# One tuned kernel of an FFT, two linear layers and a routed expert layer: single fold additions given out per step, evictions of a group moved to one engine

## The chip, the cores and the metric

The kernel runs on one core of one Trainium2 chip. The metric is the device time of one execution in microseconds, the median of several runs. A separate execution was recorded by the hardware profiler; all rows below are from that one.

## The reference

The input `x` has 8 batches of 3072 positions by 256 features. Three stages follow each other:

```python
X = np.fft.fft(x, axis=1); X = np.fft.fft(X, axis=2); x = X.real.reshape(24576, 256)
a = x @ w1; b = x @ w2; x = ((a * b) @ w3) @ w_out          # 256 -> 1024 -> 1024 -> 256
logits = x @ w_gate                                         # 8 experts
# every expert takes its 3072 best tokens, in order of the logit
out[mask_e] = np.maximum(x[mask_e] @ e1[e], 0) @ e2[e]
```

All of it is single precision. The kernel keeps that accuracy with three matmuls for one product (high times high, high times low, low times high), so most tensors exist as a rounded high part and a low part that holds the rest.

## The kernel before, in words

The program has two stages. Stage A makes the FFT and the two linear layers and leaves the rows of `x` and the logits. Stage B chooses the tokens and runs the experts. The change touches stage A alone.

Stage A works in steps. A step is one `(batch, set, q, f)`: 8 batches, 2 sets of frequencies, 3 blocks `q` of 256 columns, 8 slices `f` of the 1024 features, so 48 steps a batch and 384 in all. In this text the steps of a batch are counted 0 to 47, and a *group* is the 8 steps of one `(batch, set, q)`; the steps with f = 2 are 2, 10, 18, 26, 34 and 42. In each step `front` (line 825) has TensorE (PE) write two accumulators in PSUM, `us` and `ue` (name `l`, four banks in all, so two steps' worth); the matmul L845 is the first that writes `ue`. ScalarE (ACT) copies `us` to `qs` (L849), VectorE (DVE) makes sum and difference `pm` (L851, L852), then their product (L868); ACT rounds the product to `ah` (L862), and GpSimd (POOL) makes the rest `al` (L863). Three steps later (`LAG`) PE multiplies `ah` and `al` with the combined second weights into four accumulators `acc` (L809, L810, L813), one bank each, over the 8 slices of the group. After the eighth slice, which falls on the next group's f = 2, the four banks are copied to SBUF (`xo`): banks 0 and 2 by ACT (L920), banks 1 and 3 by DVE (L921, because `EV` is 1). There is one set of `acc` banks, so the next group's first product waits for these copies. The last 8 groups (from step 32 of batch 6) are kept aside: there PE makes logits alone, two short matmuls a step.

Beside that, the *fold* of the next batch is given out piece by piece. `fold_batch` loads three tiles of the input and adds and subtracts reflected rows, on POOL, in pieces whose costs in us it yields; the loop lets it run while a credit, which gains `FOLD` = 1.3 a step, is positive. In the third tile (t = 2) four additions per side cross the two halves of the partitions; these `shifted` additions (L348 to L351, 64x128 each) are DVE's. Then `split` makes the high part (ACT, L373) and the low part (DVE, L374) of `FA` and `FB`, and from step 38 on PE reads `FA` for the next batch's first transform (`dft_set`, matmuls into `l` between the steps' own). `later(n, fn)` puts a piece off to the end of the n-th step from now, where `due()` gives it out.

The order on each engine is the order in which this Python code records it; nothing is rescheduled.

Of the kernel before, what the change touches and what calls it, by code (L numbers as in the profile page):

```python
# [213 lines left out]
def cp(eng, out, in_):  # L214

    return eng.dma_start(f32(out), f32(in_))
# [63 lines left out]
def stage_a(ctx, tc, I, nb, k):  # L280
    nc, vec, act, pool = k.nc, k.vec, k.act, k.pool
# [36 lines left out]
    def later(n, fn):  # L318
        if late is None or n == 0:
            fn()  # L320
        else:
            late.append([n, fn])
# [9 lines left out]
    def fold_rows(xt, t, cw, new, fe, wait=0):  # L332

        lo, hi = slice(0, 64), slice(64, 128)
        if xt is not None:
            xo = xt[:, :, 0]
            for z, op in ((fe, ALU.add), (xo, ALU.subtract)):
                for h in range(2):
                    g = slice(4 * h, 4 * h + 4)
                    pool.tensor_tensor(z[:, g], xt[:, g, 0], xt[:, g, 1], op=op)  # L340
                    yield 1.2
            sides = ((fe, ALU.add, ALU.subtract, ALU.add, 0), (xo, ALU.subtract, ALU.add, ALU.subtract, 2))
        else:
            sides = ((fe, ALU.add, ALU.subtract, ALU.add, 0),)

        def shifted(z, o, opx):
            a, b = (0, 1) if o == 0 else (1, 0)
            vec.tensor_tensor(FO[lo, o], z[lo, a], z[lo, a + 2], op=opx)  # L348
            vec.tensor_tensor(FO[hi, o], z[lo, b], z[lo, b + 2], op=opx)
            vec.tensor_tensor(FO[lo, o + 1], z[hi, a], z[hi, a + 2], op=opx)  # L350
            vec.tensor_tensor(FO[hi, o + 1], z[hi, b], z[hi, b + 2], op=opx)  # L351

        for z, op4, opx, opr, o in sides:
            pool.tensor_tensor(z[:, 0:4], z[:, 0:4], z[:, 4:8], op=op4)
            yield 1.2
            if z is fe:
                FO = new()
            if t < 2:
                pool.tensor_tensor(FO[:, o:o + 2], z[:, 0:2], z[:, 2:4], op=opx)
                yield 0.7  # L360
            else:
                later(wait, lambda z=z, o=o, opx=opx: shifted(z, o, opx))
            pool.tensor_tensor(z[:, 4:6], z[:, 0:2], z[:, 2:4], op=opr)
            yield 0.7
            r = 4 + o
            first, second = (ALU.subtract, ALU.add) if o == 0 else (ALU.add, ALU.subtract)
            pool.tensor_tensor(FO[:, r], z[:, 4], z[:, 5], op=first)
            yield 0.4
            pool.tensor_tensor(FO[:, r + 1], z[:, 4], z[:, 5], op=second)
            yield 0.4  # L370

    def split(hi, lo, src):
        act.activation(hi, src, AF.Copy)  # L373
        vec.tensor_tensor(lo, src, hi, op=ALU.subtract)  # L374
# [72 lines left out]
    def xplace(dt):  # L447
        return own.tile([128, 2080], dt, name="xt", bufs=2)[:, :2048]


    def fold_batch(b, F, wait=0):
        FA = [own.tile([128, 2, 6, 128], F32R, name=f"FA{i}") for i in range(2)]
        FB = [own.tile([128, 4, 3, 128], F32R, name=f"FB{i}") for i in range(2)]
        F[b] = FA, FB
        xts = []

        def rows():

            for hl in range(2):
                r = k.sp_d[2 + 3 * hl:5 + 3 * hl, b:b + 1].rearrange("h b d -> b h d")  # L460
                cp(nc.sync, FA[hl][0:1].rearrange("p x i d -> p (x i) d")[:, 1:7:5], r[:, 0:2])
                cp(nc.sync, FB[hl][0:1, 2, 0:1], r[:, 2:3])

        def load(t):
            xts.append(xplace(F32).rearrange("p (g h d) -> p g h d", g=8, h=2))
            nc.sync.dma_start(xts[t], I["xg"][b, :, t].rearrange("p g (h d) -> p g h d", h=2))

        load(0)
        if wait:
            load(1)  # L470
        else:
            yield load
        for t in range(3):
            xt = xts[t]
            fe = fold.tile([128, 8, 128], F32, name="fe")
            made = []

            def new():
                made.append(fold.tile([128, 8, 128], F32, name="FO"))
                return made[0]  # L480

            yield from fold_rows(xt, t, 128, new, fe, wait)
            FO = made[0]
            if t == 0:
                load(2)

            fa = FO[:, 0:4].rearrange("p (x i) d -> p x i d", x=2)
            later(wait + 1 if wait else 0, lambda t=t, fa=fa: split(FA[0][:, :, 2 * t:2 * t + 2], FA[1][:, :, 2 * t:2 * t + 2], fa))
            later(wait + 2 if wait else 0, lambda t=t, FO=FO: split(FB[0][:, :, t], FB[1][:, :, t], FO[:, 4:8]))
            if t == 0:  # L490
                later(wait + 2 if wait else 0, rows)

# [207 lines left out]
    def col_mm(st):  # L700
        for step in (dft_a(0, FA8, NB, sF, tmp) if st == 0 else dft_b(0, FB8, NB, sF, tmp, r8)):
            step()
        q = (nc.scalar, nc.sync)[st]
        if st == 1:
            x = xplace(F32R)
            ehs[1] = [x[:NB, i * 768:(i + 1) * 768] for i in range(2)]
        eh = ehs[st]
        split(eh[0], eh[1], sF[:NB, 0:768])
        if st == 1:
            split(r8m[0], r8m[1], sF[:NB, 769:770])  # L710
        for r, hl in ((0, 0), (1, 0), (2, 1)):
            cp(q, k.ed[st, :, r], eh[hl])
            if st == 1:
                cp(q, k.em[r].rearrange("(b o) -> b o", o=1), r8m[hl])
        if st == 1:
            for w in range(2):
                cp(q, mb3[32 * w:32 * w + 3], k.em)
# [7 lines left out]
    EOs, F, st0 = {}, {}, []  # L725

    with tc.manual_schedule(engines=ALL):
# [7 lines left out]
        fg = fold_batch(0, F)  # L735
# [134 lines left out]
    def number(g):  # L870

        b, st, q, f = g
        return b * 6 + st * 3 + q - (nb * 6 - k.aside)
# [90 lines left out]

    e3t, acct, gates = [None, None], [None], []
    steps = [(b, st, q, f) for b, st in sets for q in range(3) for f in range(NF)]
    LAG, FOLD, EV, AH, W8 = 3, 1.3, 1, 1, 1
    FOLD_AT = 3
    LAST = (7,)
    DFT_AT = {0: (1, 4, 7, 10), 1: (14, 16, 18, 20)}  # L970
    pend, todo, fg, credit, ahp = [], [], iter(()), 0.0, []
    mid = middle()
    with tc.manual_schedule(engines=ALL):
        for t in e3s:
            vec.memset(t.rearrange("p w c -> p (w c)").bitcast(F32), 0.0)
        for g in steps:
            b, st, q, f = g
            si, at = b * 2 + st, q * NF + f
            if st == 0 and at == FOLD_AT and b + 1 < nb:
                fg = fold_batch(b + 1, F, 2)  # L980
            nx = sets[si + 1] if si + 1 < len(sets) else None
            if nx and at == (DFT_AT[st][0] if (b, st) != (0, 0) else 5):
                if st == 1:
                    assert next(fg, None) is None, 'fold late'
                EOs[nx], todo = dft_set(nx[0], nx[1], F[nx[0]])
            fr = front(g)
            if (b, st, at) == (0, 0, 0):

                cut = 2 * (576 + 579) // 2 + 63
                pool.dma_start(tabB[:, :, :cut], I["tab"][:, :, C1N:C1N + cut])  # L990
                pool.dma_start(sg, I["sg"])
                pool.dma_start(tabB[:, :, cut:], I["tab"][:, :, C1N + cut:])
            if (b, st, at) == (0, 0, 4):
                col_mm(1)
            pend.append((g, fr))
            if len(pend) > LAG:
                back(*pend.pop(0))
            fr[3]()
            ahp.append(fr[2])
            if len(ahp) > AH:  # L1000
                ahp.pop(0)()
            due()
            credit = min(credit + FOLD, FOLD)
            while credit > 0:
                credit -= next(fg, 9.0)
            if (b, st) == (nb - 1, 1) and at in (2, 4, 6, 8, 10, 12, 22):
                next(mid)
            if (b, st, at) == (NB - 1, 0, 0):
                k.load_rcon()
            if number(g) == -3 and f == 0:  # L1010
                gates.append(work.tile([128, NF, 2 * E], F32R, name="gates", bufs=1))
                for i in range(2):
                    act.activation(gates[0][:, :, i * E:(i + 1) * E], W[i][:, :, D:], AF.Copy)
            if at in (DFT_AT[st] if (b, st) != (0, 0) else (5, 7, 9, 11)) and todo:
                todo.pop(0)(W8)
        for fn in ahp:
            fn()
        for p in pend:
            back(*p)
            due()  # L1020
        while late:
            due()
# [631 lines left out]
```

## Time and profile before

| | us |
|---|---|
| median of 3 runs (2855.15 to 2857.86) | 2857.8 |
| the profiled execution | 2851.39 |
| its span, first to last instruction | 2849.6 |
| PE busy | 2681.3 (94%) |
| DVE busy | 2156.5 (76%) |
| POOL busy | 1528.8 (54%) |
| ACT busy | 1307.3 (46%) |

The first step's L845 starts at 119.0 us and the last group ends near 1416 us; stage B takes the rest. Busy shares are means over both stages. Matmuls overlap each other, so PE counts as busy as long as one is under way; what can be won on PE in stage A are the holes between them, and those are what the waits of PE list.

### The profile page before, as it was taken

The page shows a single profiled execution, that of the slowest core. Times are in us where ns is not written, and L with a number is a line of the kernel's source. Part 1 is how long each engine was busy: PE and PEld are TensorE (multiplying, and loading weights), DVE is VectorE, ACT ScalarE, POOL GpSimd, SP SyncE. Part 2 cuts the span into 40 slices and gives each one's busy share as a digit, 9 for nine tenths or more (in the row PEclk, how much of TensorE's full clock was granted, in tenths as well). Part 3 has the DMA queues.
Part 4 walks back from the last instruction along what each step waited for, and adds up shares of the span by engine and source line. Part 5 has one row for each costly group of instructions (what it writes and reads, how often), then busy time and mean ns, then how long its engine had stood idle before and what let it go on. Part 6 is the DMA issues. An engine that isn't in the chain of part 4 may idle for free.

```text
span 2849.6 us, 52085 instructions
## 1 busy us (share of the span) xinstructions
PE 2681.3 (94%) x19967; PEld 2462.0 (86%) x19967; DVE 2156.5 (76%) x3888; ACT 1307.3 (46%) x2319; POOL 1528.8 (54%) x1537
## 2 busy tenths in 40 slices
PE   4899999999999999999897899989999999999998
PEld 2899999999999999987696788878888888889997
DVE  8787787977879787898878788788787878863222
ACT  2443433434344343444453656556474646533332
POOL 7385775847658494864403335353534445353532
PEclk8999999999999999999998999999999999999999
DMA  6311010100102010135385112121211212111211
GB/s 222 122 61 39 31 53 21 60 27 31 53 16 68 16 53 31 43 135 202 133 310 185 50 63 58 43 74 41 76 46 62 55 40 77 45 64 44 75 46 36
DMA packets 104709, 207.35 MB, mean 73 GB/s; under 512 B 35179, under 2 KB 60443, under 8 KB 99339
## 3 DMA queue, kind: packets, MB, share of 16 engines
q1 hardware_dynamic: 81000, 131.02, 13.6%
q0 software_dynamic: 22224, 72.58, 8.0%
q8 instruction: 158, 2.59, 0.4%
q14 instruction: 93, 0.75, 0.1%
q10 hardware_dynamic: 1234, 0.41, 0.1%
HBM read 118.15 MB, written 80.28 MB: 70 GB/s over the span
## 4 chain that ended last, share of the span: by engine, by line
PE 69%; DVE 21%; issue 4%; ACT 3%; POOL 2%; DMA 2%; DVEq 0%; another core or an unknown queue 0%; POOLq 0%; SPq 0%; ACTq 0%
PE yp L1491 14%; PE l L220 6%; PE l L222 6%; PE l L221 6%; PE hp L220 5%; PE hp L221 4%; PE hp L222 4%; PE acc L809 4%; PE acc L813 4%; PE acc L810 4%; DVE qs L868 3%; DVE oR L1094 3%; PE l L845 2%; DVE pm L851 2%; DVE pm L852 2%
## 5 line engine op out<-in xcount | busy, mean ns | idle before, releaser
L863 POOL TENSOR_TENSOR al<-qs,ah 128x512 fp32r<-128x512 f32 x376 | 515.6, 1371 | 421.3 <-ACT ah L862 336.4
L1491 PE MATMUL yp<-FA,W 128*128 128x256 f32 x3040 | 623.7, 287 | 19.6 <-DVE W L1474 9.6
L1491 PEld LDWEIGHTS yp<-FA,W 128*128 128x128 f32 x3040 | 499.3, 191 | 46.5 <-DVE W L1474 13.6
L868 DVE TENSOR_TENSOR qs<-pm 128x512 f32<-128x512 f32 x384 | 393.9, 1026 | 36.3 <-POOL al L863 0.9
L1474 DVE SCALAR_TENSOR_TENSOR W<-hp,W 128x512 fp32r<-128x512 f32 x336 | 230.1, 687 | 229.5 <-ACT W L1470 217.2
L851 DVE TENSOR_TENSOR pm<-l,qs 128x512 f32<-128x512 f32 x384 | 264.9, 690 | 174.1 <-PE l L222 143.6
L1491 PE MATMUL yp<-FB,W 128*128 128x256 f32 x1520 | 388.6, 282 | 0.0
L849 ACT ACTIVATE qs<-l 128x512 f32<-128x512 f32 x384 | 227.7, 593 | 347.6 <-PE l L222 325.3
L862 ACT ACTIVATE ah<-qs 128x512 fp32r<-128x512 f32 x376 | 236.8, 630 | 281.4 <-DVE qs L868 237.7
L220 PE MATMUL hp<-tabA,tabB 128*128 128x512 f32 x768 | 320.5, 417 | 0.9 <-ACT tabA L1440 0.9
L1470 ACT ACTIVATE W<-hp 128x512 fp32r<-128x512 f32 x336 | 197.3, 594 | 257.9 <-PE hp L222 237.9
L221 PE MATMUL hp<-tabA,tabB 128*128 128x512 f32 x768 | 305.0, 397 | 6.0 <-DVE tabA L1444 6.0
L1501 POOL DMA_INDIRECT out_dram<-yo,oi x188 | 189.4, 1007 | 225.4 <-DMA out_dram<-yo,oi 212.2
L1491 PEld LDWEIGHTS yp<-FB,W 128*128 128x128 f32 x1520 | 288.5, 190 | 14.5
L809 PE MATMUL acc<-W,ah 128*128 128x264 f32 x1120 | 285.6, 286 | 14.3 <-DVE xo L921 14.3
L810 PE MATMUL acc<-W,ah 128*128 128x264 f32 x1120 | 284.2, 284 | 0.0
L1094 DVE TENSOR_SCALAR_CACHE_REDUCE oR<-oR,nx 128x1536 uint16<-128x1536 uint16 x196 | 281.4, 1459 | 0.0
L852 DVE TENSOR_TENSOR pm<-l,qs 128x512 f32<-128x512 f32 x384 | 261.3, 680 | 0.0
L1465 POOL TENSOR_TENSOR W<-xo,W 128x512 fp32r<-128x512 f32 x48 | 66.6, 1387 | 352.9 <-ACT W L1463 334.9
L1415 POOL DMA_INDIRECT xt<-xs_d,idx x192 | 194.6, 1013 | 111.4 <-issue 50.8
L222 PE MATMUL hp<-tabA,tabB 128*128 128x512 f32 x624 | 247.1, 396 | 0.0
L809 PEld LDWEIGHTS acc<-W,ah 128*128 128x128 f32 x1120 | 211.1, 188 | 16.5 <-DVE xo L921 16.4
(368 smaller groups left out, 7042.4 us busy)
## 6 DMA issues: line engine op xcount, KB each, us to landing
xs_d<-xo SPq DMA_DIRECT2D x96, 260.0 KB
xt<-in_xg_dram SPq DMA_DIRECT2D x24, 1024.0 KB
away<-ah SPq DMA_DIRECT2D x56, 256.0 KB
away<-al SPq DMA_DIRECT2D x56, 256.0 KB
yo<-away SPq DMA_DIRECT2D x28, 512.0 KB
raw<-in_w3t_dram SPq DMA_DIRECT2D x16, 512.0 KB
FA<-away SPq DMA_DIRECT2D x14, 512.0 KB
FB<-away SPq DMA_DIRECT2D x14, 512.0 KB
```

Source lines behind the costliest of these rows:

```text
L220: nc.tensor.matmul(out, ah, bh, start=start, stop=False, skip_group_check=True)
L221: nc.tensor.matmul(out, ah, bl, start=False, stop=False, skip_group_check=True)
L222: nc.tensor.matmul(out, al, bh, start=False, stop=stop, skip_group_check=True)
L809: nc.tensor.matmul(acc[i][:, :264], ah[:, a], W[0][:, f], start=f == 0, stop=False, skip_group_check=True)
L810: nc.tensor.matmul(acc[i][:, :264], ah[:, a], W[1][:, f], start=False, stop=False, skip_group_check=True)
L851: vec.tensor_tensor(pm[:, 0].rearrange("p w c -> p (w c)"), ue, qs, op=ALU.add)
L852: vec.tensor_tensor(pm[:, 1].rearrange("p w c -> p (w c)"), ue, qs, op=ALU.subtract)
L862: act.activation(ah, qs, AF.Copy)
L863: (vec if n == k.aside - 1 and f in LAST else pool).tensor_tensor(al, qs, ah, op=ALU.subtract)
L868: return ah, al, parts, lambda: vec.tensor_tensor(ab, pm[:, :, 0], pm[:, :, 1], op=ALU.mult)
L1094: vec.tensor_scalar(jk[:, :n], T[:, :n], nx[:, i:i + 1], None, op0=ALU.is_ge, op1=ALU.add, accum_out=acc[:, i:i + 1])
L1491: nc.tensor.matmul(yp[i], hhl[seq[s][0]][:, t[i]], seq[s][1], start=f == 0 and s == 0 and (i % 2 == 0 or len(yp) == 4), stop=f == NF - 1 a ...
```

## The change

Three edits, all in stage A. The four shifted additions of a side are no longer one deferred piece but four, given out at the end of four successive steps, and the splits of the third tile come two steps later than before to stay behind them. `EV` becomes 0: ACT copies all four banks of a group. And the fold's credit is set to -4 x 1.3 when a batch's fold begins, so that it starts in the same step in each batch.

```diff
         def shifted(z, o, opx):
             a, b = (0, 1) if o == 0 else (1, 0)
-            vec.tensor_tensor(FO[lo, o], z[lo, a], z[lo, a + 2], op=opx)
-            vec.tensor_tensor(FO[hi, o], z[lo, b], z[lo, b + 2], op=opx)
-            vec.tensor_tensor(FO[lo, o + 1], z[hi, a], z[hi, a + 2], op=opx)
-            vec.tensor_tensor(FO[hi, o + 1], z[hi, b], z[hi, b + 2], op=opx)
+            for i, (to, of, c) in enumerate(((lo, lo, a), (hi, lo, b), (lo, hi, a), (hi, hi, b))):
+                later(wait and wait + i, lambda to=to, of=of, c=c, d=o + i // 2: vec.tensor_tensor(FO[to, d], z[of, c], z[of, c + 2], op=opx))
...
-                later(wait, lambda z=z, o=o, opx=opx: shifted(z, o, opx))
+
+                shifted(z, o, opx)
...
-            later(wait + 1 if wait else 0, lambda t=t, fa=fa: split(FA[0][:, :, 2 * t:2 * t + 2], FA[1][:, :, 2 * t:2 * t + 2], fa))
-            later(wait + 2 if wait else 0, lambda t=t, FO=FO: split(FB[0][:, :, t], FB[1][:, :, t], FO[:, 4:8]))
+            later(wait + (3 if t == 2 else 1) if wait else 0, lambda t=t, fa=fa: split(FA[0][:, :, 2 * t:2 * t + 2], FA[1][:, :, 2 * t:2 * t + 2], fa))
+            later(wait + (4 if t == 2 else 2) if wait else 0, lambda t=t, FO=FO: split(FB[0][:, :, t], FB[1][:, :, t], FO[:, 4:8]))
...
-    LAG, FOLD, EV, AH, W8 = 3, 1.3, 1, 1, 1
+    LAG, FOLD, EV, AH, W8 = 3, 1.3, 0, 1, 1
...
             if st == 0 and at == FOLD_AT and b + 1 < nb:
-                fg = fold_batch(b + 1, F, 2)
+                fg, credit = fold_batch(b + 1, F, 2), -4 * FOLD
```

Line numbers of the changed kernel are one lower from here on (L868 is L867). On PE the order of the instructions is the same as before. On DVE, in batch 0 from the product of step 31 on (`FO` is the fold's output, `fe` and `xt` its two sides, `pm` and `qs` the step's own), it was:

```order
L868 TENSOR_TENSOR qs_2257<-pm_2274 128x512
L348 TENSOR_TENSOR FO_2215<-fe_2002 64x128
L349 TENSOR_TENSOR FO_2215<-fe_2002 64x128
L350 TENSOR_TENSOR FO_2215<-fe_2002 64x128
L351 TENSOR_TENSOR FO_2215<-fe_2002 64x128
L851 TENSOR_TENSOR pm_2317<-l1_2302,qs_2300 128x512
L852 TENSOR_TENSOR pm_2317<-l1_2302,qs_2300 128x512
L868 TENSOR_TENSOR qs_2300<-pm_2317 128x512
L851 TENSOR_TENSOR pm_2355<-l1_2340,qs_2338 128x512
L852 TENSOR_TENSOR pm_2355<-l1_2340,qs_2338 128x512
L868 TENSOR_TENSOR qs_2338<-pm_2355 128x512
L348 TENSOR_TENSOR FO_2215<-xt_1625 64x128
```

and the same place now:

```order
L867 TENSOR_TENSOR qs_2257<-pm_2274 128x512
L349 TENSOR_TENSOR FO_2215<-fe_2002 64x128
L850 TENSOR_TENSOR pm_2313<-l1_2298,qs_2296 128x512
L851 TENSOR_TENSOR pm_2313<-l1_2298,qs_2296 128x512
L867 TENSOR_TENSOR qs_2296<-pm_2313 128x512
L349 TENSOR_TENSOR FO_2215<-fe_2002 64x128
L850 TENSOR_TENSOR pm_2353<-l1_2338,qs_2336 128x512
L851 TENSOR_TENSOR pm_2353<-l1_2338,qs_2336 128x512
L867 TENSOR_TENSOR qs_2336<-pm_2353 128x512
L349 TENSOR_TENSOR FO_2215<-fe_2002 64x128
L349 TENSOR_TENSOR FO_2215<-xt_1625 64x128
L850 TENSOR_TENSOR pm_2392<-l1_2377,qs_2375 128x512
```

Four additions in a row behind one product became one behind each product, two where the two sides overlap (steps 33 and 34). In every one of the seven folds they now stand in steps 31, 32, 33, 33, 34, 34, 35 and 36, with the low part of `FA` in step 37 and of `FB` in step 38; before, a side's run of four stood in a step between 28 and 33 and the other's two steps later, another place in each batch, and `FA` between 32 and 37.

On ACT, at the end of a group (step 34 of batch 0: `acc0` to `acc3` are the four banks), it was:

```order
L849 ACTIVATE qs_2379<-l1_2380 128x512
L920 ACTIVATE xo_2413<-acc0_2114 128x264
L920 ACTIVATE xo_2416<-acc2_2116 128x264
L862 ACTIVATE ah_2358<-qs_2338 128x512
L849 ACTIVATE qs_2428<-l1_2429 128x512
```

and now:

```order
L848 ACTIVATE qs_2375<-l1_2376 128x512
L919 ACTIVATE xo_2409<-acc0_2114 128x264
L920 ACTIVATE xo_2409<-acc1_2115 128x264
L919 ACTIVATE xo_2412<-acc2_2116 128x264
L920 ACTIVATE xo_2412<-acc3_2117 128x264
L861 ACTIVATE ah_2356<-qs_2336 128x512
L848 ACTIVATE qs_2426<-l1_2427 128x512
```

Two copies left DVE's queue, where they stood behind the `pm` pair of step 34, and entered ACT's ahead of `ah`.

## Rows read from the trace of the kernel before

**Rows 1.** Busy time in stage A: us, then PE, PEld, DVE, ACT, POOL, clock
```profile
119.00:1282.40 1163.40, 1141.21 (x8865) 1107.54 (x8863) 942.02 (x1302) 473.50 (x861) 797.25 (x775) 1.00 0.14 48
```

**Rows 2.** Waits of PE, 119 to 1300 us: total us, times, longest
```profile
PE acc L809 <- DVE xo L921: 14.3, 9, 4.2
PE l L845 <- DVE pm L852: 3.9, 6, 0.8
PE l L845 <- issue: 2.4, 1, 2.4
...
```

**Rows 3.** Timeline of PE: start us, us, engine, line [idle before <-releaser]
```profile
225.39 0.40 PE L845 MATMUL l<-e,ew 128*128 128x512 f32 x1
228.51 0.39 PE L845 MATMUL l<-e,ew 128*128 128x512 f32 x1
...
232.57 0.47 PE L845 MATMUL l<-e,ew 128*128 128x512 f32 x1 [0.78 <-DVE pm L852]
...
239.80 0.39 PE L809 MATMUL acc<-W,ah 128*128 128x264 f32 x1 [2.72 <-DVE xo L921]
...
248.08 0.40 PE L845 MATMUL l<-e,ew 128*128 128x512 f32 x1
...
251.89 0.34 PE L222 MATMUL l<-tabA,FA 128*128 128x384 f32 x1
...
395.75 0.47 PE L845 MATMUL l<-e,ew 128*128 128x512 f32 x1 [2.37 <-issue]
...
744.83 0.59 PE L809 MATMUL acc<-W,ah 128*128 128x264 f32 x1 [4.17 <-DVE xo L921]
```

**Rows 4.** Timeline of DVE
```profile
224.83 0.69 DVE L851 TENSOR_TENSOR pm<-l,qs 128x512 f32<-128x512 f32 x1
...
227.16 1.37 DVE L348 TENSOR_TENSOR FO<-fe 64x128 f32<-64x128 f32 x1
...
231.13 0.69 DVE L851 TENSOR_TENSOR pm<-l,qs 128x512 f32<-128x512 f32 x1
...
239.32 0.76 DVE L921 COPY xo<-acc 128x264 f32<-128x264 f32 x2
...
394.97 0.68 DVE L852 TENSOR_TENSOR pm<-l,qs 128x512 f32<-128x512 f32 x1
```

**Rows 5.** Timeline of ACT, the group's copies in step 34 of batch 0
```profile
234.33 0.38 ACT L920 ACTIVATE xo<-acc 128x264 f32<-128x264 f32 x1
234.87 0.39 ACT L920 ACTIVATE xo<-acc 128x264 f32<-128x264 f32 x1 [0.16 <-PE acc L222]
```

**Rows 6.** Clock around the longest wait, columns as in Rows 1
```profile
744.00:748.00 4.00, 3.17 (x14) 3.17 (x15) 3.76 (x7) 0.63 (x1) 3.04 (x7) 0.50 0.22 66
748.00:752.00 4.00, 4.00 (x27) 3.90 (x26) 3.32 (x8) 1.12 (x2) 1.52 (x2) 0.74 0.46 120
```

**Rows 7.** Groups by line, 100 to 1300 us: count | busy us, mean ns | idle before
```profile
L868 DVE TENSOR_TENSOR qs<-pm 128x512 f32<-128x512 f32 x341 | 349.7, 1025 | 32.1 <-POOL al L863 0.9 <-DVE pm L852 0.5
L851 DVE TENSOR_TENSOR pm<-l,qs 128x512 f32<-128x512 f32 x341 | 235.2, 690 | 164.0 <-PE l L222 138.4 <-ACT ah L862 3.5 <-PE acc L222 1.3
L852 DVE TENSOR_TENSOR pm<-l,qs 128x512 f32<-128x512 f32 x341 | 232.0, 680 | 0.0
...
L921 DVE COPY xo<-acc 128x264 f32<-128x264 f32 x80 | 30.6, 423 | 0.3 <-PE acc L222 0.3
L920 ACT ACTIVATE xo<-acc 128x264 f32<-128x264 f32 x80 | 30.4, 390 | 30.4 <-PE acc L222 30.2
...
L374 DVE TENSOR_TENSOR FA<-FO,FA 128x512 fp32r<-128x512 f32 x21 | 27.5, 1308 | 0.0
...
L351 DVE TENSOR_TENSOR FO<-xt 64x128 f32<-64x128 f32 x7 | 8.8, 1263 | 0.1
...
L348 DVE TENSOR_TENSOR FO<-xt 64x128 f32<-64x128 f32 x7 | 1.9, 275 | 0.0
```

**Rows 8.** Timeline of POOL, its last fold piece in batch 0
```profile
232.22 0.45 POOL L369 TENSOR_TENSOR FO<-xt 128x128 f32<-128x128 f32 x1
```

## The prediction

> **What bounds the kernel now.** First the busy times by stretch: between the first step of stage A and the start of its last batch PE is busy 1141.2 of 1163.4 us at the full clock, DVE 942 and ACT 474 [rows 1]. So stage A goes at PE's pace, and an edit on DVE or ACT can only win back holes in PE, 22 us there at most, or open new ones. Next the waits of PE in that stretch: one line dominates, the second layer's L809, nine times held by DVE's copy L921 of a group's banks, 14.3 us together; then L845, seven times, 3.9 + 2.4 us [rows 2]. The seventh, put down to "issue", is DVE as well: PE starts at 395.75, just behind the end of DVE's `pm` (394.97 + 0.68) that frees an `l` bank [rows 3, 4]. None of the lines names a DMA.
>
> Then the timeline, for why DVE is late. In batch 0 the four shifted additions of one side begin at 227.16, and the `pm` of step 32 starts only at 231.13, 4.0 us later [rows 4]. That is 5.74 us behind its step's L845 at 225.39; PE's L845 two steps later, which needs that `pm`'s bank, stood 0.78 us [rows 3]. I call this distance d: up to d = 5.74 - 0.78, about 5.0 us, PE doesn't notice. The second side's four push the copies of step 34 to 239.32, and PE's L809 waits 2.72 us [rows 3, 4]. ACT's two copies of that same group stood at 234.33 and 234.87 [rows 5], 4.5 us ahead of DVE's, although ACT's `ah` waits for the same late products of DVE.
>
> **The evictions.** 80 copies of 423 ns leave DVE (34 us in all) and come to ACT at 390 ns (31 us) [rows 7]. Where do they lie on ACT? Behind the same step's `qs` and ahead of `ah`, which is where ACT's own two already are; those waited for PE's last product and little else (30.2 of 30.4 us idle before L920 is PE's `acc` [rows 7]). Two more make the row of four end about 0.8 us later than now: in batch 0 at 235.26 + 0.78, 236.0 instead of 239.32 + 0.76. PE asked for bank 1 at 239.80 - 2.72, 237.1 [rows 3]. So all nine L809 waits go: 14.3 us. Behind the copies on ACT stand `ah` (for POOL's `al`, which PE reads two steps, 6 us, later) and the next `qs`; both can be 0.8 us later without PE waiting. What is late next, if nothing else were done, is L845, through the same DVE; that is the second edit's part.
>
> **The shifted additions.** Nothing is removed: 56 additions (eight groups of seven, the costliest 8.8 us, the cheapest 1.9 us, 42.4 us together, 0.76 each on the mean [rows 7]). They only stand one or two behind a product instead of four. I replay batch 0, whose fold keeps its place. A step on PE is 228.51 - 225.39, 3.1 us [rows 3]. DVE's own work in a step is 0.69 + 0.68 less their overlap, some 1.4 with gaps, and the product 1.0 [rows 7], so 2.4, and 0.7 us a step is spare. `pm` of step 31 starts at 224.83 and the first addition at 227.16 for 1.37, as now [rows 4]. Then step 32's `pm` starts at 228.5 (d = 3.1 instead of 5.74). Step 32 adds 2.4 and a dear addition of 1.26, since POOL still folds: `pm` of 33 at 232.2, d = 3.7. POOL's last piece ends at 232.22 + 0.45 [rows 8]. Behind it the additions come right after a product, while POOL's `al` of that product still waits for ACT, and I price them as the cheap group, 0.28 [rows 7]. Step 33 adds 2.4 + 2 x 0.28: 235.1, d = 3.5; step 34 the same: 238.1, d = 3.4; step 35 adds 2.7: d = 3.0; step 36 the same: d = 2.6. The peak of 3.7 stays below 5.0, so the seven L845 waits go too: 6.3 us.
>
> The price of one addition is the unknown: 0.28 if alone, 1.26 if beside POOL [rows 7]. I take the cheap end for steps 33 to 36, because the groups that are cheap now are the ones that directly follow a product; the mean and the dear end are the rivals below.
>
> **What a wait costs beside itself.** The clock: after the 4.17 us hole the granted clock is 0.50 (1.2 GHz) in 744 to 748 and 0.74 in 748 to 752 [rows 6]; half of 3.17 us and a quarter of 4 are 2.6 us at most, and 2.0 taken, as DVE was still behind there. The first matmul after a wait is some 0.1 us longer (0.47 for 0.39 to 0.40 at L845 [rows 3]); 16 times, 1.6 us.
>
> **The credit.** It moves the starts of the six later folds by a few steps, with POOL's pieces, the splits and the loads of `xt` on SP's queue, ahead of or behind the small loads of `e`. Each fold then stands as batch 0's does, where none of PE's waits lies before step 31, so I cost it at nothing. One place is not covered: in the last fold (batch 6) two additions and the two splits now fall in steps 35 to 38, where PE's steps are short because the groups are kept aside and DVE has no spare. Two additions at 0.28 to 1.26 and two splits at 1.31 [rows 7] are at most 5.1 us of DVE; the transform's matmuls from step 38 on hide some of it or all. Bounds 0 and 5.1; I take 2, nearer to nothing, since POOL's fold is over there.
>
> **The sum.** 14.3 + 6.3 + 2.0 + 1.6 - 2 = 22.2 us. Stage B begins when the last logits are there and is unchanged, so the end moves by the same 22: the profiled execution goes from 2851.4 to 2829. The runs shown have a median 6.4 above it; taken from 2857.8, the forecast is 2836 us.
>
> **Rivals.**
> *The wait moves to the transform.* If an addition costs its mean, 0.76, step 37's `pm` is reached at 228.5 + 5 x 2.4 + 7 x 0.76 = 245.8, against its L845 at 240.9: d = 4.9. The low part of `FA` follows 2.4 + 1.31 later [rows 7], 8.6 us after that L845. The transform's ninth matmul, the first that reads it, comes 3.1 + (251.89 - 248.08) = 6.9 after it [rows 3]. PE waits 1.7 us in each of seven folds, 12 us: 2848. For it: the mean is what the trace has. Against: it holds the dear ones in a run of four.
>
> *The bank wait only changes its line.* If DVE stays as late as now in half the cases, PE, no longer stopped at L809, runs into L845: in batch 0 by some 0.5 us, behind the 4.17 us wait by some 2. Half of 14.3 then comes back: 2843. Against: DVE has two copies less to do exactly there.
>
> *Slower: every addition waits for a whole POOL instruction.* At 1.26 each, step 37's `pm` comes at 228.5 + 12 + 8.8 = 249.3, d = 8.4. PE stands 3.4 us at L845 and, with d held at 5.0, 1.8 at the transform; 5.2 x 7 = 36 us against 22 won: 2872. The point from which it turns is 22 / 7 = 3.2 us of new waits a fold, which is near 1.0 us an addition. For it speaks the last of the `xt` run, 1263 ns, against 275 for the first [rows 7].
> The Trainium skill (SBUF — State Buffer, Who interferes with whom) says that a DVE instruction with two SBUF inputs contends with a GpSimd instruction that reads SBUF, and that the one that issued first keeps the shared port for its whole length. By that rule, which speaks against handing out single instructions, each of the eight can lose a whole POOL instruction, and this rival's time would come out. The trace agrees with it in kind, since 275 and 1263 ns are the same operation; how often an addition meets POOL it does not say.
>
> **Chances.** The forecast 0.68 (2829 to 2843), the transform 0.14, the other line 0.10, every addition dear 0.04, no effect at all or something unseen 0.04. A difference under 0.2%, 5.7 us, is what a measurement of this kernel can't tell from none; so faster is below 2852. That gives 0.89 faster, 0.07 the same, 0.04 slower. The range, with the first three cases in it, is 2828 to 2850.
>
> **What would show it.** Right: no PE wait of L809 on a copy, ACT's four copies within 2 us of the last product, `pm` never more than 5 us behind its L845 in steps 31 to 37, and no half clock inside stage A after its start. Wrong: PE waits in the transform of step 38 on the split's low part, L845 waits longer than now, additions near 1.26 throughout, or a longer batch 6.

## The result and the profile after

The changed kernel takes 2828.45 us (2827.68 to 2830.8, four runs) beside 2857.83 (2855.15 to 2859.85) for the kernel before, 29.4 us between the medians; the ratio is 0.9906, interval 0.9895 to 0.9918, that is 27 us less, between 23 and 30. A second set of four runs gives 0.9898 (0.9881 to 0.9916). The profiled execution took 2827.68 us with a span of 2825.9. The forecast was 2836 with a range from 2828 to 2850: the median lies 0.45 us inside its lower end.

Where the time went: I call *stage A* the stretch from the first step's L845 (L844 now) to the last step's. It went from 1296.7 us (119.0 to 1415.7) to 1271.6 (118.8 to 1390.4), 25.1 us less; the rest of the span got 1.4 us longer, with no edit in it. PE does the same matmuls in the stretch of [rows 1], now 25.3 us shorter. Its holes there fell from 22.2 us to 2.0, and it is busy for 5.1 us less (1141.2 to 1136.1):

```profile
118.80:1256.90 1138.10, 1136.12 (x8865) 1104.78 (x8864) 936.46 (x1222) 499.20 (x941) 793.82 (x775) 1.00 0.15 50
```

The waits of PE between 119 and 1300 us, all that are left; they answer to [rows 2]:

```profile
PE l L222 <- DVE FA L373: 1.1, 1, 1.1
PE acc L898 <- ACT xo L900: 0.5, 1, 0.5
PE l L844 <- DVE pm L851: 0.3, 1, 0.3
PE l L844 <- ACT qs L848: 0.2, 1, 0.2
```

No wait of L808 (L809 before) for a bank copy is left, and 0.3 us for `pm`. The one new line, 1.1 us, is the last fold's. L898 belongs to the logits of the groups kept aside, and the kernel before has the same 0.5 us there (at L899).

The granted clock is 1.00 in all of batches 0 to 6. In the last batch it fell once, 2 us behind a wait of 0.95 us at L898 (columns as in [rows 1]):

```profile
1316.00:1320.00 4.00, 4.00 (x20) 3.49 (x19) 3.67 (x5) 1.83 (x3) 1.91 (x2) 0.58 0.52 197
```

DVE in batch 0 from step 31 on, as in [rows 4] (start us, us, line):

```profile
227.25 1.37 DVE L349 TENSOR_TENSOR FO<-fe 64x128 f32<-64x128 f32 x1
228.54 0.67 DVE L850 TENSOR_TENSOR pm<-l,qs 128x512 f32<-128x512 f32 x1
...
231.05 1.27 DVE L349 TENSOR_TENSOR FO<-fe 64x128 f32<-64x128 f32 x1
232.33 0.69 DVE L850 TENSOR_TENSOR pm<-l,qs 128x512 f32<-128x512 f32 x1
...
234.88 0.29 DVE L349 TENSOR_TENSOR FO<-fe 64x128 f32<-64x128 f32 x1
235.18 0.28 DVE L349 TENSOR_TENSOR FO<-xt 64x128 f32<-64x128 f32 x1
235.39 0.68 DVE L850 TENSOR_TENSOR pm<-l,qs 128x512 f32<-128x512 f32 x1
...
238.16 0.69 DVE L850 TENSOR_TENSOR pm<-l,qs 128x512 f32<-128x512 f32 x1
...
240.58 0.69 DVE L850 TENSOR_TENSOR pm<-l,qs 128x512 f32<-128x512 f32 x1
...
243.25 0.69 DVE L850 TENSOR_TENSOR pm<-l,qs 128x512 f32<-128x512 f32 x1
```

The `pm` of step 32 starts at 228.54 instead of 231.13, and the six starts of steps 32 to 37 lie within 0.3 us of the prediction's replay (228.5, 232.2, 235.1, 238.1, 240.8, 243.5). Every addition stands behind a product or another addition. The first two run beside POOL's fold and `al` and cost 1.37 and 1.27 us; the other six, with POOL idle or only copying, 0.28 to 0.32.

Not every fold goes that way. In batches 1, 3, 4 and 6 the first two cost 0.55 and 0.71, and the dear one is the first of `xt`, in step 33, beside POOL's `al`; in batch 1:

```profile
397.58 0.44 DVE L349 TENSOR_TENSOR FO<-fe 64x128 f32<-64x128 f32 x1
398.03 1.29 DVE L349 TENSOR_TENSOR FO<-xt 64x128 f32<-64x128 f32 x1
```

The order on DVE and on POOL is the same in all seven folds, and in the second profile of this kernel it is batches 2, 3 and 6 that go the second way. So the order alone does not settle which additions meet POOL. The prediction's d is at most 4.2 us in steps 31 to 37 of the first kind of fold and 3.7 of the second.

ACT at the group's end in step 34, answering to [rows 5]:

```profile
232.94 0.39 ACT L919 ACTIVATE xo<-acc 128x264 f32<-128x264 f32 x1 [0.66 <-PE acc L222]
233.32 0.39 ACT L920 ACTIVATE xo<-acc 128x264 f32<-128x264 f32 x1
233.70 0.39 ACT L919 ACTIVATE xo<-acc 128x264 f32<-128x264 f32 x1
234.07 0.39 ACT L920 ACTIVATE xo<-acc 128x264 f32<-128x264 f32 x1
```

The four banks are free 1.5 us after the row of copies begins; [rows 4] had the last one at 240.08. The groups of the two edits, as in [rows 7] (count | busy us, mean ns | idle before):

```profile
L867 DVE TENSOR_TENSOR qs<-pm 128x512 f32<-128x512 f32 x349 | 390.9, 1120 | 37.5 <-DVE pm L851 1.4 <-POOL xo L925 0.5
L920 ACT ACTIVATE xo<-acc 128x264 f32<-128x264 f32 x80 | 31.5, 394 | 0.0
L919 ACT ACTIVATE xo<-acc 128x264 f32<-128x264 f32 x80 | 31.4, 392 | 17.6 <-PE acc L222 17.6
L349 DVE TENSOR_TENSOR FO<-fe 64x128 f32<-64x128 f32 x28 | 17.6, 630 | 0.7
L349 DVE TENSOR_TENSOR FO<-xt 64x128 f32<-64x128 f32 x28 | 12.1, 433 | 0.6
```

The 56 additions now take 29.7 us instead of 42.4, 0.53 each instead of 0.76, and the copies of [rows 7] took 34 us of DVE that are gone. But the product rose from 1025 ns to 1120 on the mean, 32 us over 341 products, and DVE is busy 936.5 us in the stretch of [rows 1] instead of 942.0. What the edits changed is when DVE is late, hardly how much it does. The product's rise comes with the evictions (1075 ns with them alone) and with the reset (1062 with it alone), not with the spreading (1023); its cause was not followed.

### The profile page after: what moved, and what is told of

Its sections match the earlier page's. It is cut to its first block, busy times and chain, and to the rows that moved or that the text cites. A ratio compares the mean times of both kernels' runs of the same rounds, so it can differ in the third digit from the quotient of the medians.

```text
span 2825.9 us, 51980 instructions
## 1 busy us (share of the span) xinstructions
PE 2679.5 (95%) x19967; PEld 2463.0 (87%) x19967; DVE 2146.9 (76%) x3808; ACT 1334.1 (47%) x2399; POOL 1529.0 (54%) x1537
## 4 chain that ended last, share of the span: by engine, by line
PE 73%; DVE 17%; ACT 3%; issue 2%; POOL 2%; DMA 1%; another core or an unknown queue 0%; SPq 0%; DVEq 0%; POOLq 0%; ACTq 0%
PE yp L1490 13%; PE l L220 7%; PE l L222 7%; PE l L221 7%; PE acc L812 5%; PE acc L808 5%; PE acc L809 5%; PE hp L220 4%; PE hp L221 4%; PE hp L222 4%; DVE oR L1093 4%; PE l L844 3%; DVE W L1473 2%; ACT ja L1088 2%; PE yp L1378 2%
## 5 line engine op out<-in xcount | busy, mean ns | idle before, releaser
L867 DVE TENSOR_TENSOR qs<-pm 128x512 f32<-128x512 f32 x384 | 427.5, 1113 | 40.8 <-DVE pm L851 1.4
L861 ACT ACTIVATE ah<-qs 128x512 fp32r<-128x512 f32 x376 | 237.1, 631 | 350.0 <-DVE qs L867 310.0
L808 PE MATMUL acc<-W,ah 128*128 128x264 f32 x1120 | 283.7, 284 | 0.0
L809 PE MATMUL acc<-W,ah 128*128 128x264 f32 x1120 | 283.3, 284 | 0.0
L1088 ACT ACTIVATE ja<-oR,nx 128x1536 bf16<-128x1536 uint16 x98 | 154.5, 1577 | 143.2 <-DVE cur L1123 112.6
```

Of the source, the lines that this page charges most:

```text
L808: nc.tensor.matmul(acc[i][:, :264], ah[:, a], W[0][:, f], start=f == 0, stop=False, skip_group_check=True)
L809: nc.tensor.matmul(acc[i][:, :264], ah[:, a], W[1][:, f], start=False, stop=False, skip_group_check=True)
L867: return ah, al, parts, lambda: vec.tensor_tensor(ab, pm[:, :, 0], pm[:, :, 1], op=ALU.mult)
```

## The experiments

Three edits make eight combinations: the kernel before, the full change, and six between them, each compared with the kernel before on the same chip. Of the kernels below, the first four in the order of the text shared one chip (before: 2857.34 us), the next four another, where the kernel before takes 2838.65, and the last three went beside one of 2856.05; so only ratios are compared across them. "Us won" below is one minus the ratio, of 2857. Stage A is that of one profiled execution each: two of the kernel before differ by 3.2 us (1296.7 and 1299.9), two of the full change by 0.2. "Additions" is the spreading with the later splits; without the reset it needs a bound on the fold's start, described below.

| kernel | ratio | interval | us won | stage A, us |
|---|---|---|---|---|
| before, again | 0.9996 | 0.9982 to 1.0010 | 1 | 1299.9 |
| evictions | 0.9955 | 0.9941 to 0.9969 | 13 | 1288.9 |
| reset | 1.0031 | 1.0018 to 1.0045 | -9 | 1311.0 |
| additions | 0.9943 | 0.9925 to 0.9960 | 16 | 1283.4 |
| evictions, reset | 0.9979 | 0.9970 to 0.9988 | 6 | 1290.7 |
| additions, reset | 0.9933 | 0.9920 to 0.9947 | 19 | 1281.6 |
| evictions, additions | 0.9909 | 0.9894 to 0.9924 | 26 | 1274.5 |
| all three | 0.9906 | 0.9895 to 0.9918 | 27 | 1271.6 |

**The kernel before, again.** No edit.

> The kernel before, unchanged, profiled a second time. The first profile has 14.3 us of PE waits of L809 and 6.3 us of L845 in stage A and a span of 2849.6 us, while its runs have a median of 2857.8. Theory 1: the late points of DVE are the same in every execution, the holes are set by the program: L809 12 to 17 us, span within 4 us of 2849.6. Theory 2: which additions meet POOL differs from one execution to the next, so the holes do too: another count or sum of L809 waits by more than 5 us, and a span nearer to the runs' 2857.

Stage A took 1299.9 us after 1296.7, with 11.9 us of waits at L809 (nine again, as in [rows 2]) and 8.4 at L845; together 20.3 instead of 20.6. So the sum of the holes belongs to the program, theory 1, though L809's sum falls just under its 12, and its bound on the span failed: 2859.9 is 10.3 us off, not 4. Something of theory 2 is there as well: in batch 0 the last `xt` addition took 0.29 us where it had taken 1.41, and the wait at L809 behind it 1.52 us instead of 2.72.

The 3.2 us of stage A are PE at a lower clock. Its waits are no longer, but it is busy 3.3 us more before the last batch, and the granted clock fell in two more places there, where the first profile has 1.00 (columns as in [rows 1]):

```profile
394.70:398.10 3.40, 3.40 (x15) 3.31 (x16) 3.16 (x5) 1.13 (x3) 1.28 (x1) 0.50 0.02 5
1074.00:1077.40 3.40, 3.40 (x17) 3.35 (x16) 3.25 (x6) 1.05 (x3) 2.05 (x2) 0.51 0.04 10
```

The other 10.3 - 3.2 = 7 us came behind stage A, where PE is busy 5.4 us more, again at a lower mean clock (the first profile, then this one):

```profile
1415.70:2849.60 1433.90, 1338.69 (x9924) 1199.56 (x9922) 997.54 (x2266) 732.84 (x1270) 604.32 (x643) 0.98 0.24 74
1418.70:2859.90 1441.20, 1344.10 (x9923) 1204.08 (x9921) 995.34 (x2266) 734.06 (x1270) 604.45 (x643) 0.97 0.23 74
```

So the first profile was a fast execution, 6.4 us under its runs' median, and gains are better read in stage A's stretch than in the span. Why the clock falls in more places in one execution than in another stays open.

**Evictions alone.**

```diff
-    LAG, FOLD, EV, AH, W8 = 3, 1.3, 1, 1, 1
+    LAG, FOLD, EV, AH, W8 = 3, 1.3, 0, 1, 1
```

> Only the evictions (all four banks by ACT; additions in runs of four, no reset). Theory 1 (the bank wait ends PE's hole): L809 has no wait any more; the late DVE shows at L845 instead in the worst places only (about 0.5 us in batch 0, 2 us in batch 3), so 13 us are won of the change's 22 to 29. Theory 2 (the wait only changes its line): L845 waits grow from 6.3 to 13 us or more and 6 to 8 us are won. Theory 3 (ACT is late): waits on ACT appear and nothing is won.

13 us were won by the ratio (9 to 17); stage A is 7.8 us shorter than in the first profile of the kernel before and 11.0 than in the second. The waits of PE in stage A:

```profile
PE l L845 <- DVE pm L852: 8.8, 9, 2.6
PE l L845 <- issue: 3.5, 2, 2.3
```

L809 is gone, as theory 1 said; but L845 doubled, from 6.3 to 12.3 us, nearer to theory 2's 13 than to 2.5 us more. Both were half right: with the copies on ACT the bank of `acc` no longer stops PE, and the same late DVE stops it one resource later. In batch 3 the 4.17 us at L809 became 2.11 at L845.

**The reset alone.**

```diff
-                fg = fold_batch(b + 1, F, 2)
+                fg, credit = fold_batch(b + 1, F, 2), -4 * FOLD
```

> Only the reset of the credit: every fold stands where batch 0's stands. Theory 1: every batch then has batch 0's holes (0.8 us at L845, 2.7 us at L809), 7 x 3.5 = 25 us against 21 and its half clock now: between 4 us slower and 2 us faster, no measurable difference. Theory 2 (the place of the fold is what matters): 5 us or more either way, with waits that differ from batch to batch.

9 us were lost, more than theory 1's bound. Its step "batch 0's holes in every batch" failed in their sizes, and in batch 0 itself, whose wait at L845 is 1.77 us now instead of 0.78: the reset puts one of POOL's fold pieces (L367 of `xt`) a step later there. PE's waits grew at both lines:

```profile
PE acc L809 <- DVE xo L921: 16.0, 11, 2.7
PE l L845 <- DVE pm L852: 13.6, 10, 1.8
```

DVE in step 31 of batch 1 shows what the place costs:

```profile
394.64 1.38 DVE L348 TENSOR_TENSOR FO<-fe 64x128 f32<-64x128 f32 x1
396.03 1.28 DVE L349 TENSOR_TENSOR FO<-fe 64x128 f32<-64x128 f32 x1
397.32 0.73 DVE L350 TENSOR_TENSOR FO<-fe 64x128 f32<-64x128 f32 x1
398.07 1.29 DVE L351 TENSOR_TENSOR FO<-fe 64x128 f32<-64x128 f32 x1
399.37 0.69 DVE L851 TENSOR_TENSOR pm<-l,qs 128x512 f32<-128x512 f32 x1
```

The run of four takes 4.7 us; batch 0's in the kernel before took 4.0 [rows 4]. The 0.7 us more are the fourth addition, 1.29 us here. They fall behind the 5.0 us at which PE begins to wait, so they count in full. PE's two waits there:

```profile
400.80 0.48 PE L845 MATMUL l<-e,ew 128*128 128x512 f32 x1 [1.73 <-DVE pm L852]
...
408.03 0.39 PE L809 MATMUL acc<-W,ah 128*128 128x264 f32 x1 [2.63 <-DVE xo L921]
```

Batch 0 of the kernel before had 0.78 and 2.72 [rows 3]. In batches 0 to 5 the `pm` of step 32 is 6.65 to 6.73 us behind its L845 and PE's wait 1.70 to 1.77: d less the wait is 4.96 each time, so the 5.0 is not a number of one place. In batches 2 to 5 the clock also went to 1.2 GHz for 3.4 us each. With runs of four, this place was a bad one for every batch of this profile.

**The additions alone.** The spreading and the later splits are those of the full change; of their lines only the additions' is shown. A fold that would start later than step 7 starts in step 7.

```diff
+                later(wait and wait + i, lambda to=to, of=of, c=c, d=o + i // 2: vec.tensor_tensor(FO[to, d], z[of, c], z[of, c + 2], op=opx))
...
-                fg = fold_batch(b + 1, F, 2)
+                fg, credit = fold_batch(b + 1, F, 2), max(credit, -4 * FOLD)
```

> Only the additions one by one, with the splits of the third tile two steps later; DVE copies banks 1 and 3 as before. Each fold keeps its place, except that one which would start later than step 7 starts in step 7 (batch 3; there the low part of FA would otherwise come behind the transform that reads it). Theory 1: the waits behind runs of four go (10 of 14.3 us at L809, all 6.3 at L845, the half clock), those behind the splits of the first two tiles stay (three L809 waits, 4 us): 17 to 19 us won. Theory 2 (the additions lose as much to POOL one by one as in a run): the sum of late DVE is the same, under 8 us won.

16 us were won (13.3 of stage A), in theory 1's manner: one by one the additions took 30.0 us instead of 42.4, and L845 nearly went. L809 kept more than I expected:

```profile
PE acc L808 <- DVE xo L920: 10.1, 9, 1.8
PE l L844 <- DVE pm L851: 1.3, 2, 0.9
```

There are nine short waits where I had three: DVE's copies stand behind whatever else DVE has in the step, a split, a fold addition or a product, and they have only some 2 us: in batch 0 of the kernel before PE's last product of the group ends at 235.2 and PE asks for bank 1 at 237.1.

**Evictions and reset, no spreading.** Both diffs above.

> Evictions on ACT and the reset, additions in runs of four: what the spreading is worth in the full change. Theory 1: batch 0's pattern in every batch, L845 waits of 0.8 at step 34 and about 0.5 at step 36, no L809 waits: 7 x 1.3 = 9 us of waits remain, 16 us won against before, 7 to 9 less than the full change. Theory 2 (ACT's copies are all that counts): as fast as the full change.

6 us were won, not 16. L845 alone held PE for 11.8 us (ten waits, the longest 2.0), and the clock fell to a half for 3.4 us in four places inside the batches. Theory 1's pattern is there in batches 3, 4 and 5, with waits of 0.8 and 0.5 to 0.6 us; in batches 0, 1, 2 and 6, with the same order on the engines, one wait of 1.8 to 2.0 stands instead, and these four are the places of the half clock. Its sizes came from batch 0 of the kernel before, which had the cheaper run of four. What the spreading is worth in the full change is 21 us, not 9.

**Additions and reset, copies shared with DVE.**

> Additions one by one and the reset, DVE copies banks 1 and 3: what the evictions are worth in the full change. Theory 1: in step 34 DVE is some 2.5 us behind, and with two copies of 0.42 us on it PE waits about 1 us at L809 in each of seven folds: 7 us less than the full change. Theory 2 (with the additions apart DVE is in time for its copies): no L809 wait, as fast as the full change.

```profile
PE acc L808 <- DVE xo L920: 9.7, 12, 1.1
PE l L222 <- DVE FA L373: 1.1, 1, 1.1
```

19 us, 8 less than the full change, with waits of up to 1.1 us at L808: theory 1. Twelve waits instead of seven, since the copies of other groups come late as well.

**Evictions and additions, no common place.** `max(credit, -4 * FOLD)` as above.

> Evictions on ACT and additions one by one, each fold in its own place, but none starting later than step 7: what the reset is worth beyond that bound. Theory 1: nothing, or up to 2 us in its favour without the reset, since batch 6's fold then ends before the short steps (its waits of 1.1 us in the transform and 0.3 us at L845 go): within 3 us of the full change. Theory 2 (one place suits all batches better): 5 us or more slower than the full change.

0.9909, the full change's time; theory 1. The folds' places then differ again, with waits of 1.6 us at L844 and 1.5 at POOL's `al`, against 0.3 and none: 3 us of stage A, within what the times can tell. The bound itself was not left out in any run. By the code it is needed: the low part of `FA` stood as late as step 37 and comes two steps later now, behind step 38, from which PE reads it.

**Every fold two steps earlier.** `-2 * FOLD` instead of `-4 * FOLD`.

> The full change with the credit set to -2 x 1.3 instead of -4 x 1.3: every fold two steps earlier. Theory 1: batch 6's wait in the transform (1.1 us) and its L845 wait (0.3 us) go, POOL's waits of 0.2 us at the second layer's al may move: 0 to 3 us faster than the full change. Theory 2: the splits of the second tile now meet the group's copies and PE waits come back: slower by more than 3 us.

0.9909 (0.9894 to 0.9924), stage A 1271.7 us against 1271.6. Batch 6 took 154.5 us instead of 155.0 and its wait in the transform went; L844's waits on ACT's `qs` came up by 0.7 us elsewhere. No difference that counts.

**The last fold alone earlier.**

```diff
-                fg, credit = fold_batch(b + 1, F, 2), -4 * FOLD
+                fg, credit = fold_batch(b + 1, F, 2), (-2 if b == nb - 2 else -4) * FOLD
```

> The full change, with the last fold alone (batch 6) set two steps earlier: credit -2 x 1.3 there, -4 x 1.3 elsewhere. Theory: its additions and splits then end by step 36, the transform finds FA written, and the 1.1 us wait in the transform and the 0.3 us at L845 go; batch 6 takes 154.5 us as with all folds two steps earlier, instead of 155.0; 0.5 to 2 us, which the times alone can't tell from none. Rival: those waits are set by the short steps themselves and come back at another line.

0.9889 (0.9871 to 0.9906) beside 0.9898 for the full change on the same chip: not told apart by the times. The waits:

```profile
PE l L844 <- ACT qs L848: 1.2, 4, 0.4
PE acc L898 <- ACT xo L900: 0.5, 1, 0.5
PE l L844 <- DVE pm L851: 0.2, 1, 0.2
```

The transform's wait is gone, as the theory said, and 1.0 us came back at L844 behind `qs`, as the rival said; batch 6 took 154.4 us. Its stage A is the shortest of the kernels, by 0.4 to 0.6 us, and no more.

**Two additions in a step.**

```diff
-                later(wait and wait + i, lambda to=to, of=of, c=c, d=o + i // 2: vec.tensor_tensor(FO[to, d], z[of, c], z[of, c + 2], op=opx))
+                later(wait and wait + i // 2, lambda to=to, of=of, c=c, d=o + i // 2: vec.tensor_tensor(FO[to, d], z[of, c], z[of, c + 2], op=opx))
```

> The full change, with the four additions of a side given out two in a step, in two steps instead of four; the splits where the full change has them. Theory 1 (what follows a product directly is cheap, whether one or two, and what counts is that no product has four behind it): DVE's pm stays under 5 us behind its step's L845, no L845 waits in batches 0 to 5, the mean addition near the full change's 0.53 us, same time as the full change within 3 us. Theory 2 (each further addition in a row meets POOL's next instruction): the mean addition rises to 0.7 or more, L845 waits of 0.3 to 0.8 us come back in most folds, 3 to 6 us slower than the full change.

0.9898 (0.9880 to 0.9915), the full change's ratio on that chip: theory 1 for the time. The first pair of batch 0 and the `pm` behind it:

```profile
227.40 2.67 DVE L349 TENSOR_TENSOR FO<-fe 64x128 f32<-64x128 f32 x2
230.09 0.69 DVE L850 TENSOR_TENSOR pm<-l,qs 128x512 f32<-128x512 f32 x1
...
232.50 0.91 DVE L349 TENSOR_TENSOR FO<-fe 64x128 f32<-64x128 f32 x2
...
235.42 0.57 DVE L349 TENSOR_TENSOR FO<-xt 64x128 f32<-64x128 f32 x2
```

The mean addition was 0.59 us, between the two theories' figures. `pm` of step 32 came 1.5 us later than with single ones, 4.8 us behind its L844 at 225.3, and that of step 33 5.0 us behind its own at 228.4: just what PE can bear. The largest d in batches 0 to 5, 5.1 us in batch 3, has no wait either. The 0.7 us of waits behind `pm` that this kernel has at L844 lie in batch 6's short steps. So it is the peak of d against 5.0 that decides: two in a row still fit, four do not.

**The full change, again.**

> The full change again, unchanged, beside the two others on the same chip: 0.990 of the kernel before by every theory, with the same waits of PE in stage A as its first profile (1.1 us in the transform, none at L809, 0.3 us behind pm at L845).

0.9898, stage A 1271.8 us, and the same waits to 0.1 us, with 0.2 us more at POOL's `al`.

## Why the prediction was right

The path was right: *PE bounds stage A and its holes are all there is to win* (stage A gave 25.1 us, the span behind it nothing); *all nine L809 waits go* (they did, 14.3 us); *the L845 waits go* (6.0 of 6.3). Of its signs, `pm` is nowhere more than 4.2 us behind in steps 31 to 37, and the four copies end 1.5 us after they begin. One sign failed: the half clock left the place of the 4.17 us wait, but a new stretch of it stands in the last batch, at 1316.

The replay of DVE is within 0.3 us at six places of batch 0; d peaks at 4.0 there (`pm` of step 33 at 232.33, its L844 at 228.3) where 3.7 stood. Its price list is right by luck in part. The reason given for 0.28, that the cheap additions are those directly behind a product, does not fit [rows 4], where the 1.37 us one at 227.16 stands directly behind a product as well. And the places priced dear and cheap are those of batches 0, 2 and 5 alone; in the other four folds the addition that cost 1.29 was one of the priced 0.28. The eight together took 4.4 us in batch 0 and 4.2 in batch 1, so that the mean of 56, 0.53 us, still meets the replay's 0.54. Nor did batch 0 quite keep its place: the reset put one POOL piece a step later.

In the stretch of [rows 1], 25.3 us shorter, the sum's terms measure as follows. The last fold was charged 2 us; its new waits are 1.1 in the transform and 0.3 at L844, 1.4 together. Waits of 1.1 us for POOL's `al` and 0.4 for ACT's `qs`, which come behind those shown in [rows 2], went too and stood in no term. All holes together gave 20.2 us where 18.6 stood (14.3 + 6.3 - 2). PE's busy time fell by 5.1 where 2.0 for the clock and 1.6 for the first matmuls stood: 2.3 in batch 3, the only one with a half clock before, and 2.8 in the other six batches, 0.5 each on the mean. So the clock was near its 2.0, and what a wait costs beside itself was twice the 1.6; why was not followed.

That explains 25 us and not the 29 between the medians. The 22.2 were read from one fast profile and taken from a median 6.4 us above it; the second profile of the kernel before has a stage A 3.2 us longer with half-clock stretches that the first lacks. How much of the 4 us is that was not measured. The measured median lies just outside the 2829 to 2843 of the forecast's own case, and 0.45 us inside the range: the mechanism was right, the hit at the edge was luck.

Of the rivals, *the wait moves to the transform* came in one fold of seven, the last, and not for the rival's reason, additions at their mean price: it is the case of the short steps, which the charge covers. *The bank wait only changes its line* is what the evictions do alone, in part: 6.0 us of 14.3 came back at L845. *Every addition dear* did not come: additions became cheaper.

What the prediction did not have is how the edits lean on each other. Alone, evictions win 13, additions 16 and the reset loses 9; pairs give 6, 19 and 26. The reason is in two allowances: PE notices DVE only when `pm` starts more than 5.0 us behind its step's L845, or when DVE's copies come more than some 2 us behind the group's last product. Evictions lift the second, spreading keeps DVE under the first. The 5.0 belongs to full steps: in batch 6's short steps 34 and 35 PE waited from a d of 3.0 to 4.3 us on. The reset wins nothing that the times can tell on top of the other two; it keeps the longer fold ahead of its reader, as the bound does.

Open: what settles which of POOL's instructions an addition meets, since two executions of one kernel differ in it; this was read from the timelines, not varied by itself. Open too: why PE's clock falls in more places in one execution than in another, and what made the product dearer.

## What to carry to other kernels

When an off-path engine stops the bounding one, find how late it may be before anything is felt, and compare peaks with that, not busy shares: cutting one long run into pieces won 16 us with no instruction less, and in the full change DVE's busy time hardly moved. Before a buffer's release is moved to a freer engine, ask which buffer the same late engine holds next; here that second hold took back 6 of 14 us until the lateness itself was cut. And a single edit's worth can depend on the others: the reset lost 9 us alone and nothing beside the other two, so undo edits from the full change as well as adding them to the old one.

## What the runs showed of the hardware

The same 64x128 addition on DVE took 0.27 to 0.32 us with POOL idle or only copying, and up to 1.44 beside POOL's additions and `al`, so its time against POOL's work mattered more than its size; and the same order on both engines gave either price, from fold to fold and from one execution to the next. The copy of 128x264 from PSUM took 392 ns on ACT and 423 on DVE, so the copy itself cost no more; but with the copies gone from DVE its product went from 1025 to 1075 ns. Within batches 0 to 6 PE's granted clock fell to 0.50 (1.2 GHz) in or just behind waits of 1.8 to 4.2 us, and not behind each of them: in the kernel before, 2.72 us in batch 0 had no fall, and the 2.4 at 395 had one in the second execution alone. In the kernels with spread additions, whose waits there are at most 1.8 us, it never fell, while in the last batch of the changed kernel it fell behind 0.95 us. And the kernel before took 0.7% less on the second chip (2838.65 for 2857.34 us). Stage A was not what differed: with all folds two steps earlier it took 1271.7 us there, and the full change 1271.6 here, while the spans were 2811.0 and 2825.9.
